# Third product of a three-stage network: one pass over the weights per token group instead of two, weights of four pairs read back from DRAM, and a one-pass PReLU on ScalarE

## The chip, the cores and the metric

The kernel runs on one core of a Trainium2 chip. The time is device microseconds of one execution; lower is better. The engines are TensorE (PE; PEld is its weight load), VectorE (DVE), ScalarE (ACT), GpSimd (POOL) and SyncE (SP), which issues nearly all DMAs. Each engine works through its own list of instructions in order.

## The reference

Decayed causal attention (4 batches, 8 heads, 576 tokens, 64 channels) gives a matrix x of 2304 tokens by 512 channels. Two feed-forward layers follow:

```python
h = x @ w_in;  g = h * sigmoid(1.702 * h);   x = g @ w_out      # first layer: products 1 and 2
h = x @ w_in;  g = max(h, 0) + alpha * min(h, 0);  g @ w_out    # second layer: products 3 and 4
```

with d_model = 512, d_ff = 2048, and alpha one number per column of h, that is per partition of the transposed h that the kernel holds. The result keeps the precision of float32.

## The kernel before

Every operand of a matmul is split in two float32r halves ("hi" by a cast, "lo" by a subtraction), and each product is three matmuls (hi·hi, hi·lo, lo·hi). All matmuls run at 128 rows of weights and 256 to 512 columns.

The order of all instructions is not written by hand. Each operation is given to a planner with its possible engines, its duration by a cost formula, what it reads and writes, and a priority; the planner places, again and again, the operation that can start first, and hands out buffers of the pools as they come free. What it emits is fixed: at run time each engine follows its list, and a late result delays whatever stands behind it. `a_sub` (lo halves, sums and differences) lets the planner choose GpSimd or VectorE; `a_copy` (hi halves) ScalarE or VectorE; `hold` ties an operation to a place in the plan.

The stages after the attention, with the times of their first matmuls in the profile:

- Product 1 (L1151), interleaved with the attention, up to 367 us. The last 768 tokens of it go through the **tail** (367 to 437 us): a Strassen-Winograd scheme (`pair`), seven products of 6 matmuls with 384 columns in place of eight. VectorE there also makes sums and differences of weights (td, tb) and prepares the weights of product 2.
- Product 2 (L1395), 437 to 627 us. Its first matmuls are placed between those of the tail. Its operands go through the tiles lh and ll (hi and lo) and lx.
- **Product 3** (L1174), 627 to 810 us, again `pair`: three groups of 768 tokens, and eight pairs of weight blocks. A pair's weights (7 combinations, hi and lo) fill one slot of the pool wS, which has 6 slots of 1,792 KB. Weights TS[0] to TS[7] are made one after the other. As only six fit, the groups are gone through twice: groups 0, 1, 2 with pairs 0 to 3, then groups 2, 1, 0 with pairs 4 to 7. The operands of a group (`group_x`: four loads of y1scr, four sums and differences at L1480, seven casts and seven subtractions) are made anew at each change of group: five times, since group 2 stands twice in a row. They lie in two pools of 3 and 4 slots.
- Product 4 (L1568), from 810 us. While product 3 runs, the weights of W2[0] to W2[2] are prepared for it.

In `pair`, three banks of PSUM are taken out of a pool of six: products 1 and 2 go to ba, 6, 7 and 4 to bb, 5 and 3 to bd, with copies (c1, u2, c5, by ScalarE at L512) and additions (by VectorE at L1203) between them. Each of the four outputs then goes through `prelu`: two ScalarE passes, relu(-h) and relu(h) (L1188, L1189), and one VectorE instruction (L1192) that adds the first, times -alpha, to the second. For the outputs o11 and o21 the passes read the bank itself; for o22 and o12 an addition has brought h to SBUF first. A bank comes free for a later product when its last reader is done.

Of the kernel before, what the change touches and what calls it, by code (L numbers as in the profile page):

```python
# [7 lines left out]
F32 = mybir.dt.float32  # L8
F32R = mybir.dt.float32r
# [15 lines left out]
SLAG = 1000.0  # L25
# [222 lines left out]
def kernel(  # L248
# [249 lines left out]
    def c_dve(n, fast=False):  # L498
        return n / (1.92 if fast else 0.96) + 68.0
# [668 lines left out]
    def product(j, x, weights, out, st, pri):  # L1168
        rd, wt = weights(TIDX[j])

        def mm(e):
            for c in range(2):
                for i, (a, b) in enumerate(((0, 0), (0, 1), (1, 0))):
                    nc.tensor.matmul(  # L1174
                        out.ap[:, :XH], wt(a, c), x.ap[:, b, c, :],
                        start=(st and c == 0 and i == 0), stop=(c == 1 and i == 2), skip_group_check=True,
                    )

        plan.add([("PE", 6 * c_mm(XH))], mm, [*rd, (x, (0, 0)), (x, (0, 1))], [out], pri)

    def prelu(o, src, mi, vp):

        tm = Buf(p_tm)
        ps = src is not None
        read = lambda: src.ap[:, :XH] if ps else o.ap

        def two(e):
            nc.scalar.activation(tm.ap, read(), AF.Relu, scale=-1.0)  # L1188
            nc.scalar.activation(o.ap, read(), AF.Relu)  # L1189

        plan.add([("ACT", 2 * c_act(XH, ps))], two, [src] if ps else [], [tm, o], vp)
        plan.add([("DVE", c_dve(XH), 0.0, True)], lambda e: nc.vector.scalar_tensor_tensor(o.ap, tm.ap, alpha_sb[:, mi:mi + 1], o.ap, op0=ALU.mult, op1=ALU.add), [tm, b_alpha], [o], vp)  # L1192

    def pair(weights, x, tmp, p_o, store, pri, vp, ms=None):
# [35 lines left out]
        store(o12, 1, 0, vp)  # L1230
        product(4, x[4], weights, bb, False, pri)
        fin(o21, bb, 0)
        store(o21, 0, 1, vp)

    def tail():
# [117 lines left out]
    for x, t in pend:  # L1353
        chunk2(x)
        advance(t)
    tail()


# [84 lines left out]
    for p in range(NPAIR):  # L1443
# [14 lines left out]
        for j, (n, src, sb_, o) in enumerate((  # L1458
# [5 lines left out]
            halves(n, src, sb_, lambda sw=sw, q=q, n=n: sw.ap[:, q:q + n], lambda sw=sw, q=q, n=n: sw.ap[:, WSLOT // 2 + q:WSLOT // 2 + q + n], sw, j, pri)  # L1464

    PART = (0, 0, 1, 2, 2, 2, 2)

    def group_x(t0, pri):
        rd = [(b_y1, (i, d)) for i in crossing(t0, GRP, in_turn) for d in range(KT)]
# [11 lines left out]

        def operand(src, pool):
            xo = Buf(pool)
            halves(2 * XH, lambda: full(src), [src], lambda: flat(xo.ap[:, 0]), lambda: flat(xo.ap[:, 1]), xo, 0, pri)
            return xo

        o = {}
        o[1] = operand(a["11"], p_xs[0])
        comb(s1, a["21"], a["22"], ALU.add)
        comb(s2, s1, a["11"], ALU.subtract)  # L1490
        o[6] = operand(s2, p_xs[0])
        o[2] = operand(a["12"], p_xs[0])
        o[5] = operand(s1, p_xs[1])
        comb(a["21"], a["11"], a["21"], ALU.subtract)
        o[7] = operand(a["21"], p_xs[1])
        comb(s2, a["12"], s2, ALU.subtract)
        o[3] = operand(s2, p_xs[1])
        o[4] = operand(a["22"], p_xs[1])
        return o

    n_it = 0
    for half in range(2):
        for gi in range(len(groups)) if half == 0 else reversed(range(len(groups))):
            t0 = groups[gi][0]
            base = 6000.0 + 100 * n_it
            if n_it != len(groups):
                x = group_x(t0, base - 150)
            for p in range(half * NPAIR // 2, (half + 1) * NPAIR // 2):
                def weights(t, p=p):
                    w = lambda: TS[p].ap.rearrange("p (a q c n) -> p a q c n", a=2, q=7, c=2)  # L1510
                    return [(TS[p], (PART[t], 0)), (TS[p], (PART[t], 1))], lambda a, c: w()[:, a, t, c, :]

                def store(src, mi, hf, vp, p=p, gi=gi, t0=t0):
                    m, s0 = p + mi * NPAIR, t0 + hf * XH
                    plan.add(DMA(P * XH * 4), lambda e: nc.sync.dma_start(h2scr[:, m, s0:s0 + XH], src.ap), [src], [(b_g2, (2 * gi + hf, m))], vp, SLAG)

                pair(weights, x, p_t, p_go, store, base + p, base + p - 50, (p, p + NPAIR))
            n_it += 1

# [12 lines left out]
    XIDX = {1: 0, 2: 2, 3: 6, 4: 1, 5: 3, 6: 4, 7: 5}  # L1532
    out_turn = [blocks[j] for j in (3, 2, 1, 0, 4)]
    g2_parts = [(i * XH, XH) for i in range(NT // XH)]
# [105 lines left out]
```

## Time and profile before

| | |
|---|---|
| time, median of 3 runs | 997.55 us (997.09 to 998.46) |
| time of the profiled execution | 997.22 us |
| its span, first to last instruction | 995.4 us |
| TensorE busy | 969.7 us (97%) |
| VectorE busy | 796.3 us (80%) |
| ScalarE busy | 635.5 us (64%) |
| granted clock of TensorE, mean | 0.997 |
| DMA | 161.27 MB, 162 GB/s |

The profiled execution's time is the span and 1.8 us around it. Busy TensorE is the union of its instructions; as matmuls overlap, a stretch is best read by how many start in it.

### The profile page before, as it was taken

How to read it: one execution, taken by the hardware profiler on the slowest of the kernel's cores; microseconds unless marked ns; L12 is line 12 of the kernel's file. 1: busy time of each engine (PE TensorE's matmuls, PEld its weight loads, DVE VectorE, ACT ScalarE, POOL GpSimd, SP SyncE). 2: the span in 40 equal slices, each digit the busy share in tenths (PEclk: the TensorE clock that was granted, in tenths of full speed). 3: DMA queues.
4: the chain of work that ended last, by engine and by line, in shares of the span. 5: the costliest groups of instructions: out<-in, count | busy, mean ns of one | idle time of the engine just before them, and what ended most of it. 6: DMA issues, size and time to landing. Idle time of an engine off the chain costs nothing.

```text
span 995.4 us, 18576 instructions
## 1 busy us (share of the span) xinstructions
PE 969.7 (97%) x6469; PEld 897.3 (90%) x6469; DVE 796.3 (80%) x1692; ACT 635.5 (64%) x1297; POOL 143.6 (14%) x277
## 2 busy tenths in 40 slices
PE   8899999999999998999999999999999999999998
PEld 6678888999998998998888988999899999999998
DVE  4778978889899789965558885688998886888976
ACT  6577744777656558866668795678988963433332
POOL 4132223443222101200000000000100000000000
PEclk9899999999999999999999999999999999999999
DMA  7666652333432125667887675544444497544423
GB/s 140 152 172 196 155 128 69 77 76 88 92 86 69 41 82 195 202 188 247 302 309 275 221 255 190 169 151 159 151 145 171 174 353 269 155 120 135 139 81 100
DMA packets 180830, 161.27 MB, mean 162 GB/s; under 512 B 99088, under 2 KB 156576, under 8 KB 179456
## 3 DMA queue, kind: packets, MB, share of 16 engines
q1 hardware_dynamic: 180720, 160.07, 52.7%
q8 instruction: 51, 0.84, 0.4%
q14 instruction: 43, 0.35, 0.1%
q10 hardware_dynamic: 16, 0.01, 0.0%
HBM read 103.51 MB, written 56.51 MB: 161 GB/s over the span
## 4 chain that ended last, share of the span: by engine, by line
PE 70%; DVE 12%; ACT 11%; issue 4%; DMA 2%; POOL 0%; SPq 0%; DVEq 0%; ACTq 0%; POOLq 0%
PE bk L1568 18%; PE bk L1395 18%; PE bk L1151 9%; PE bk L1174 9%; PE bk L1004 3%; PE bk L1072 3%; ACT lx L1188 2%; PE bk L1067 2%; PE bk L1027 2%; ACT lx L1189 2%; DVE bk L942 1%; PE bk L928 1%; ACT lx L512 1%; DMA lx<-h1scr 1%; PE bk L998 1%
## 5 line engine op out<-in xcount | busy, mean ns | idle before, releaser
L1174 PE MATMUL bk<-x,wS 128*128 128x384 f32 x1008 | 178.6, 336 | 4.3 <-DVE lx L1203 3.0
L1174 PEld LDWEIGHTS bk<-x,wS 128*128 128x128 f32 x1008 | 174.1, 188 | 8.7 <-ACT lx L512 4.0
L1151 PE MATMUL bk<-xh,w 128*128 128x256 f32 (+1 forms) x640 | 158.4, 313 | 3.4 <-ACT w L512 3.0
L1395 PE MATMUL bk<-lh,w 128*128 128x512 f32 (+1 forms) x640 | 146.9, 368 | 0.0
L1395 PEld LDWEIGHTS bk<-lh,w 128*128 128x128 f32 x640 | 112.7, 189 | 19.8
L1151 PEld LDWEIGHTS bk<-xh,w 128*128 128x128 f32 x640 | 112.0, 191 | 9.9 <-issue 3.5
L1151 PE MATMUL bk<-xl,w 128*128 128x256 f32 (+1 forms) x320 | 98.0, 306 | 1.5 <-DVE xl L517 1.5
L512 ACT CAST x<-x 128x768 fp32r<-128x768 f32 (+2 forms) x73 | 60.3, 857 | 58.2 <-PE bk L1568 43.8
L517 DVE TENSOR_TENSOR ll<-lx,lh 128x512 fp32r<-128x512 f32 (+1 forms) x79 | 50.7, 642 | 49.5 <-PE bk L1395 43.3
L942 DVE CUSTOM_DVE_ANT_0 bk<-bk,mask 128x512 f32<-128x512 f32 (+4 forms) x160 | 75.1, 490 | 12.1 <-PE bk L928 5.2
L1085 ACT ACTIVATE e<-bk 128x384 f32<-128x384 f32 (+3 forms) x192 | 62.0, 393 | 34.8 <-PE bk L1072 18.5
L517 DVE TENSOR_TENSOR x<-x,x 128x768 fp32r<-128x768 f32 (+2 forms) x73 | 70.1, 981 | 16.7 <-ACT x L512 16.0
L1395 PE MATMUL bk<-ll,w 128*128 128x512 f32 (+1 forms) x320 | 81.3, 368 | 0.1
L1192 DVE SCALAR_TENSOR_TENSOR lx<-lx,alpha_sb 128x384 f32<-128x384 f32 x96 | 61.7, 651 | 13.4 <-ACT lx L1189 12.6
L1568 PE MATMUL bk<-wS,x 128*128 128x256 f32 x567 | 70.6, 283 | 0.0
L1568 PEld LDWEIGHTS bk<-wS,x 128*128 128x128 f32 x567 | 69.2, 192 | 0.0
L1568 PE MATMUL bk<-wS,lh 128*128 128x256 f32 x378 | 68.7, 283 | 0.0
L1395 PEld LDWEIGHTS bk<-ll,w 128*128 128x128 f32 x320 | 57.0, 189 | 10.1 <-DVE ll L517 0.3
L1362 ACT ACTIVATE lx<-lx 128x512 f32<-128x512 f32 (+1 forms) x80 | 46.8, 588 | 29.6 <-DVE ll L517 26.7
L512 ACT CAST lh<-x 128x768 fp32r<-128x768 f32 (+3 forms) x38 | 31.6, 857 | 51.1 <-PE bk L1568 43.2
L1151 PEld LDWEIGHTS bk<-xl,w 128*128 128x128 f32 x320 | 61.1, 191 | 2.3 <-DVE xl L517 1.9
L1568 PEld LDWEIGHTS bk<-wS,lh 128*128 128x128 f32 x378 | 59.0, 192 | 0.0
(231 smaller groups left out, 2128.6 us busy)
## 6 DMA issues: line engine op xcount, KB each, us to landing
h2scr<-lx SPq DMA_DIRECT2D x96, 192.0 KB
wraw<-in_moe_w_in_dram SPq DMA_DIRECT2D x32, 512.0 KB
wraw<-in_moe_w_out_dram SPq DMA_DIRECT2D x32, 512.0 KB
lx<-h1scr SPq DMA_DIRECT2D x64, 256.0 KB
x<-h2scr SPq DMA_DIRECT2D x32, 512.0 KB
w2scr<-wS SPq DMA_DIRECT2D x5, 1792.0 KB
x<-y1scr SPq DMA_DIRECT2D x20, 384.0 KB
h1scr<-gg SPq DMA_DIRECT2D x48, 128.0 KB
```

Of the source, the lines that this page charges most:

```text
L512: nc.scalar.copy(dst, src)
L517: E[e].tensor_tensor(dst, a, b, op=ALU.subtract)
L942: plan.add([("DVE", c_dve(c1 - c0))], lambda e, pm=pm, c0=c0, c1=c1, mk=mk, m0=m0, col=col, f0=f0: nc.vector.tensor_tensor_reduce(pm.ap[:, ...
L1004: nc.tensor.matmul(pb[hh].ap[:, c0:c1], vr.ap[:, t, hh, :], e32.ap[:, hh, e0:e0 + m], start=st, stop=sp, skip_group_check=True,)
L1072: nc.tensor.matmul(pss[hh].ap[:w, o_:o_ + m], x.ap[r, a:a + w], y.ap[r, s0 - q0:n], start=i == 0, stop=i == 3, skip_group_check=True)
L1085: plan.add([("ACT", c_act(x1 - x0, True))], lambda e, hh=hh, pss=pss, e32=e32, w=w, x0=x0, x1=x1: nc.scalar.activation(e32.ap[:w, hh, :x1 ...
L1151: nc.tensor.matmul(ph.ap[:, :n], w.ap[:, a, c, :], x[c // 2].ap[:, c % 2, :n], start=(c == 0 and j == 0), stop=(c == KT - 1 and j == 2))
L1174: nc.tensor.matmul(out.ap[:, :XH], wt(a, c), x.ap[:, b, c, :], start=(st and c == 0 and i == 0), stop=(c == 1 and i == 2), skip_group_chec ...
L1192: plan.add([("DVE", c_dve(XH), 0.0, True)], lambda e: nc.vector.scalar_tensor_tensor(o.ap, tm.ap, alpha_sb[:, mi:mi + 1], o.ap, op0=ALU.mu ...
L1362: plan.add([("ACT", c_act(n))], lambda e: nc.scalar.activation(g.ap[:, :n], raw.ap[:, :n], AF.Gelu_apprx_sigmoid), [raw], [g], pri)
L1395: nc.tensor.matmul(py[d].ap[:, :n], w[:, a, d * P:(d + 1) * P], (lo if x else h).ap[:, :n], start=(k == 0 and (a, x) == (0, 0)), stop=(k = ...
L1568: nc.tensor.matmul(py[j].ap[:, t * HF:(t + 1) * HF], x.ap[:, q:q + P], w[:, o, a, :], start=(k == 0 and t == 0 and c == 0), stop=(k == NPA ...
```

## The change

- **Once per group.** Product 3 goes once through groups 0, 1, 2, with all eight pairs in each, in turned order: 0 to 7, then 2 to 7, 0, 1, then 4 to 7, 0 to 3. `group_x` runs three times in place of five.
- **Weights read back.** During group 0, TS[0] to TS[3] are copied to a DRAM tensor tscr (four DMAs of 1,792 KB, gated by the last product of pairs 0, 2, 4, 6). Groups 1 and 2 read two of them back each, into slots that have come free. TS[6] and TS[7] take the slots of TS[0] and TS[1], and are made during group 0.
- **Operand slots.** Two more slots (p_xe) lie in lh and ll, which product 2 has left. Group 1's operands 1 and 6 go there; a table SLOT says where each goes.
- **PReLU.** One ScalarE pass r = relu(-h) (now L1195) and one VectorE instruction h + (1 - alpha) r (L1196); alpha is turned into 1 - alpha once. For o11 and o21 VectorE reads h from the bank.
- **No GpSimd** for operations planned after the tail (`late`).
- Product 4 takes its token blocks in the order 0 to 4 (before: 3, 2, 1, 0, 4).

```diff
+    SLOT = ({1: 0, 6: 0, 2: 0, 5: 1, 7: 1, 3: 1, 4: 1}, {1: 2, 6: 3, 2: 0, 5: 0, 7: 1, 3: 1, 4: 1}, ...)
+    p_xe = [st(nm, F32R, LH, [4 * XH], 0, after=[p_str[q]]) for nm, q in (("lh", "qh"), ("ll", "ql"))]
...
     def a_sub(n):
+        if late:
+            return [("DVE", c_dve(n), 0.0, True)]
         return [("POOL", c_pool(n), 0.0, True), ("DVE", c_dve(n), BS + WS * n, True)]
...
-        def two(e):
-            nc.scalar.activation(tm.ap, read(), AF.Relu, scale=-1.0)
-            nc.scalar.activation(o.ap, read(), AF.Relu)
-        plan.add([("ACT", 2 * c_act(XH, ps))], two, [src] if ps else [], [tm, o], vp)
-        plan.add([("DVE", c_dve(XH), 0.0, True)], lambda e: nc.vector.scalar_tensor_tensor(o.ap, tm.ap, alpha_sb[:, mi:mi + 1], o.ap, op0=ALU.mult, op1=ALU.add), [tm, b_alpha], [o], vp)
+        tm = o if ps else Buf(p_tm)
+        h = lambda: src.ap[:, :XH] if ps else o.ap
+        plan.add([("ACT", c_act(XH, ps))], lambda e: nc.scalar.activation(tm.ap, h(), AF.Relu, scale=-1.0), [src] if ps else [o], [tm], vp)
+        plan.add([("DVE", c_dve(XH), 0.0, not ps)], lambda e: nc.vector.scalar_tensor_tensor(
+            o.ap, tm.ap, alpha_sb[:, mi:mi + 1], h(), op0=ALU.mult, op1=ALU.add
+        ), [tm, b_alpha, *([src] if ps else [])], [o], vp)
...
     tail()
+    late.append(True)
...
+    for p in range(KEPT):
+        keep.append(plan.add(DMA(P * WSLOT * 4), lambda e, p=p, x=TS[p]: nc.sync.dma_start(tscr[:, p], x.ap.bitcast(F32)), [TS[p]], [(b_ts, p)], 5000.0 + p))
...
-    for half in range(2):
-        for gi in range(len(groups)) if half == 0 else reversed(range(len(groups))):
-            if n_it != len(groups):
-                x = group_x(t0, base - 150)
-            for p in range(half * NPAIR // 2, (half + 1) * NPAIR // 2):
+    for gi in range(len(groups)):
+        x = group_x(t0, base - 150, gi)
+        for n_p in range(NPAIR):
+            p = (2 * gi + n_p) % NPAIR
+            if gi and n_p >= NPAIR - 2:
+                TS[p] = Buf(wS)
+                plan.add(DMA(P * WSLOT * 4), lambda e, p=p, x=TS[p]: nc.sync.dma_start(x.ap.bitcast(F32), tscr[:, p]), [(b_ts, p)], [TS[p]], base + n_p - 5)
...
+            if gi == 0 and n_p % 2 == 0:
+                hold(keep[n_p // 2], o)
```

The instructions of each engine stand in another order afterwards. Three places follow: the change of group (on two engines), the weights TS[6], and the tail.

TensorE, at the change from group 0 to the next group. In the names, bk is a bank, x, lh and ll hold operands, and wS_… is a weight slot. Before, slot 5505 is that of pair 3 of group 0, and 5813 of pair 0 of group 1:

```order
L1174 MATMUL bk_85<-x_6594,wS_5505 128x384 x6
L1174 MATMUL bk_90<-x_6558,wS_5813 128x384 x6
L1174 MATMUL bk_88<-x_6639,wS_5505 128x384 x6
L1174 MATMUL bk_91<-x_6643,wS_5505 128x384 x6
L1174 MATMUL bk_89<-x_6558,wS_5813 128x384 x6
L1174 MATMUL bk_90<-x_6594,wS_5813 128x384 x6
```

And now, with 5239 the slot of pair 7 of group 0, and 5345 of pair 2 of group 1:

```order
L1183 MATMUL bk_93<-x_6595,wS_5239 128x384 x6
L1183 MATMUL bk_86<-lh,wS_5345 128x384 x6
L1183 MATMUL bk_87<-x_6643,wS_5239 128x384 x6
L1183 MATMUL bk_88<-ll,wS_5345 128x384 x6
L1183 MATMUL bk_86<-x_6559,wS_5345 128x384 x6
L1183 MATMUL bk_90<-x_6641,wS_5239 128x384 x6
L1183 MATMUL bk_92<-x_6559,wS_5345 128x384 x6
L1183 MATMUL bk_90<-x_6643,wS_5239 128x384 x6
L1183 MATMUL bk_88<-x_6641,wS_5345 128x384 x6
```

The first two products of the new group read lh and ll, and its products that need an x slot of the old group come later.

VectorE, at the same change. Before (x are operand halves and their sums; lx outputs of `pair`; one of the four sums and differences of L1480 stands on GpSimd's list here):

```order
L517 TENSOR_TENSOR x_6558<-x_6537,x_6558 128x768
L1203 TENSOR_TENSOR bk_88<-bk_88,lx 128x384
L517 TENSOR_TENSOR x_6558<-x_6537,x_6558 128x768
L517 TENSOR_TENSOR x_6639<-x_6575,x_6639 128x768
L517 TENSOR_TENSOR x_6594<-x_6575,x_6594 128x768
L1480 TENSOR_TENSOR x_6537<-x_6575,x_6537 128x768
L1192 SCALAR_TENSOR_TENSOR lx<-lx,alpha_sb 128x384
L517 TENSOR_TENSOR x_6639<-x_6537,x_6639 128x768
L517 TENSOR_TENSOR x_6643<-x_6537,x_6643 128x768
L1203 TENSOR_TENSOR lx<-bk_88,lx 128x384
L1203 TENSOR_TENSOR lx<-bk_91,lx 128x384
```

And now:

```order
L523 TENSOR_TENSOR x_6595<-x_6538,x_6595 128x768
L523 TENSOR_TENSOR x_6643<-x_6538,x_6643 128x768
L1209 TENSOR_TENSOR bk_88<-bk_88,lx 128x384
L1209 TENSOR_TENSOR lx<-bk_90,lx 128x384
L1209 TENSOR_TENSOR lx<-bk_87,lx 128x384
L523 TENSOR_TENSOR x_6641<-x_6538,x_6641 128x768
L1196 SCALAR_TENSOR_TENSOR lx<-lx,alpha_sb 128x384 x2
L1495 TENSOR_TENSOR x_6538<-x_6576 128x768
L1495 TENSOR_TENSOR x_6538<-x_6538 128x768
L1495 TENSOR_TENSOR x_6576<-x_6538,x_6576 128x768
L523 TENSOR_TENSOR x_6643<-x_6538,x_6643 128x768
```

Fewer subtractions stand in a row ahead of the additions that free banks, and sums and differences, now those of group 2, stand on VectorE.

ScalarE, where the weights TS[6] go into the slot that TS[0] leaves; wc and tt hold the new weights before their split. Before (slot wS_5813):

```order
L512 COPY lx<-bk_88 128x384
L512 CAST wS_5813<-wc_536 128x512
L512 CAST wS_5813<-tt_5245 128x1024
L691 ACTIVATE wc_554<-wraw_414 128x512
L1188 ACTIVATE lx<-bk_87 128x384
L1189 ACTIVATE lx<-bk_87 128x384
L692 ACTIVATE wraw_414<-wraw_414 128x512
L512 COPY lx<-bk_92 128x384
```

And now (slot wS_5814):

```order
L1195 ACTIVATE lx<-bk_90 128x384
L518 COPY lx<-bk_87 128x384
L518 CAST wS_5814<-wc_537 128x256
L518 CAST wS_5814<-wc_555 128x512
L518 CAST wS_5814<-tt_5246 128x1024
L700 ACTIVATE wc_537<-wraw_415 128x512
L1195 ACTIVATE lx<-bk_93 128x384
L701 ACTIVATE wraw_415<-wraw_415 128x512
L518 COPY lx<-bk_86 128x384
```

In the kernel before, the slot's last readers are matmuls; now its readers include the copy of the slot to tscr. The copies out of banks (COPY) stand behind the casts in both.

TensorE, in the tail (tb and w hold weights there). Before, matmuls of product 2 (L1395) stand between the products of the tail:

```order
L1174 MATMUL bk_88<-xt_4432,tb_4409 128x384 x6
L1174 MATMUL bk_86<-xt_4366,tb_4513 128x384 x6
L1174 MATMUL bk_85<-xt_4372,tb_4513 128x384 x6
L1174 MATMUL bk_88<-xt_4327,w_944 128x384 x6
L1395 MATMUL bk_89<-lh,w_102 128x512 x2
L1395 MATMUL bk_90<-lh,w_102 128x512 x2
L1395 MATMUL bk_92<-lh,w_102 128x512 x2
L1395 MATMUL bk_87<-lh,w_102 128x512 x2
L1174 MATMUL bk_86<-xt_4418,tb_4513 128x384 x6
```

And now, at the same products:

```order
L1183 MATMUL bk_89<-xt_4432,tb_4409 128x384 x6
L1183 MATMUL bk_87<-xt_4366,tb_4512 128x384 x6
L1183 MATMUL bk_86<-xt_4372,tb_4512 128x384 x6
L1183 MATMUL bk_89<-xt_4327,w_944 128x384 x6
L1183 MATMUL bk_87<-xt_4418,tb_4512 128x384 x6
```

Ahead of the last pair's products, 20 matmuls of product 2 stood in the tail (8, 4 and 8); now 8 do, and the rest stand at its end.

## Rows read from the trace of the kernel before

**Rows 1.** Windows by stage: us, busy PE/PEld/DVE/ACT/POOL (x), PEclk, DMA, GB/s.

```profile
364.00:437.00 73.00, 70.47 (x387) 67.31 (x387) 69.19 (x123) 58.56 (x108) 10.25 (x12) 1.00 0.59 191
...
627.00:809.00 182.00, 177.72 (x1006) 173.32 (x1005) 158.90 (x268) 151.86 (x319) 10.88 (x8) 1.00 0.52 171
```

**Rows 2.** The same view, third product cut in stretches of 30 us.

```profile
660.00:690.00 30.00, 28.42 (x162) 27.63 (x161) 24.33 (x36) 23.21 (x50) 2.49 (x1) 1.00 0.43 142
690.00:720.00 30.00, 28.17 (x159) 26.94 (x158) 27.71 (x51) 26.28 (x57) 5.25 (x4) 1.00 0.47 160
720.00:750.00 30.00, 29.26 (x163) 27.83 (x162) 28.25 (x52) 26.99 (x58) 3.14 (x3) 1.00 0.47 150
750.00:780.00 30.00, 30.00 (x174) 29.90 (x174) 25.94 (x42) 25.50 (x54) 0.00 (x0) 1.00 0.44 152
780.00:809.00 29.00, 28.87 (x165) 28.06 (x164) 26.81 (x52) 24.70 (x52) 0.00 (x0) 1.00 0.75 256
```

**Rows 3.** Line L1174: duration ns min/median/max, first and last start us.

```profile
L1174 PE MATMUL bk<-x,wS x1008: 333/334/446, 627.1 to 809.6; 128*128 128x384 f32 x168
```

**Rows 4.** Timeline, TensorE, first group change: start us, us [idle <-releaser].

```profile
654.70 11.18 PE L1174 MATMUL bk<-x,wS 128*128 128x384 f32 x63
667.29 2.35 PE L1174 MATMUL bk<-x,wS 128*128 128x384 f32 x12 [1.42 <-DVE lx L1203]
```

**Rows 5.** Timeline, VectorE, first group change.

```profile
661.25 1.14 DVE L1192 SCALAR_TENSOR_TENSOR lx<-lx,alpha_sb 128x384 f32<-128x384 f32 x2
...
664.05 2.72 DVE L1192 SCALAR_TENSOR_TENSOR lx<-lx,alpha_sb 128x384 f32<-128x384 f32 x2
666.70 1.01 DVE L1203 TENSOR_TENSOR lx<-bk,lx 128x384 f32<-128x384 f32 x2
```

**Rows 6.** Timeline, GpSimd, first group change: start us, us.

```profile
663.34 2.49 POOL L1480 TENSOR_TENSOR x<-x 128x768 f32<-128x768 f32 x1 [104.95 <-DVE x L517]
```

**Rows 7.** VectorE by line and form, 627 to 809: busy, mean ns.

```profile
L1192 DVE SCALAR_TENSOR_TENSOR lx<-lx,alpha_sb 128x384 f32<-128x384 f32 x93 | 59.9, 652 | 13.4 <-ACT lx L1189 12.6
L517 DVE TENSOR_TENSOR x<-x,x 128x768 fp32r<-128x768 f32 x32 | 29.5, 952 | 3.9 <-ACT x L512 3.5
L1203 DVE TENSOR_TENSOR lx<-bk,lx 128x384 f32<-128x384 f32 x47 | 25.3, 551 | 5.1 <-PE bk L1174 4.8 <-ACT lx L1188 0.2
...
L517 DVE TENSOR_TENSOR wS<-tt,wS 128x1024 fp32r<-128x1024 f32 x5 | 6.1, 1221 | 0.5 <-ACT wS L512 0.5
...
L694 DVE CUSTOM_DVE_ANT_0 wc<-wraw,wc 128x1024 uint16<-128x1024 uint16 x6 | 4.1, 684 | 0.0
L517 DVE TENSOR_TENSOR wS<-wc,wS 128x512 fp32r<-128x512 f32 x5 | 3.4, 683 | 0.0
...
L517 DVE TENSOR_TENSOR wS<-wc,wS 128x256 fp32r<-128x256 f32 x5 | 2.1, 419 | 0.0
```

**Rows 8.** ScalarE by line and form, 627 to 809: busy, mean ns.

```profile
L512 ACT COPY lx<-bk 128x384 f32<-128x384 f32 x72 | 34.2, 489 | 5.5 <-DVE bk L1203 3.9 <-PE bk L1174 1.3
...
L1188 ACT ACTIVATE lx<-bk 128x384 f32<-128x384 f32 x47 | 23.3, 496 | 0.6 <-PE bk L1174 0.6
```

**Rows 9.** Queue of SyncE, timeline: a copy of one weight slot to DRAM.

```profile
529.80 0.32 SPq L1440 DMA_DIRECT2D w2scr<-wS  x1
```

**Rows 10.** Windows of 1 us around that copy.

```profile
531.00:532.00 1.00, 1.00 (x6) 0.84 (x5) 0.23 (x1) 0.74 (x2) 0.00 (x0) 1.00 1.06 422
...
535.00:536.00 1.00, 1.00 (x6) 0.82 (x5) 1.00 (x3) 0.75 (x3) 0.00 (x0) 1.00 0.89 297
```

**Rows 11.** Windows of 1 us, weight slots being read back.

```profile
796.00:797.00 1.00, 1.00 (x7) 0.81 (x6) 1.00 (x3) 1.00 (x3) 0.00 (x0) 1.00 0.68 149
```

**Rows 12.** Timeline, GpSimd, in the tail.

```profile
373.61 1.44 POOL L517 TENSOR_TENSOR w<-wc,w 128x512 fp32r<-128x512 f32 x1 [23.27 <-ACT w L512]
```

**Rows 13.** Timeline, VectorE, in the tail.

```profile
373.81 1.78 DVE L1285 TENSOR_TENSOR tw<-w 128x512 f32<-128x512 f32 x1
```

**Rows 14.** Timeline, TensorE, in the tail.

```profile
376.45 1.66 PE L1174 MATMUL bk<-xt,tb 128*128 128x384 f32 x8 [0.84 <-DVE got L1203]
```

More of the change, by code (lines that the diff above doesn't have):

```diff
@@ L296 @@
     SPILL = 3
+    KEPT = 4
     HF = 256
@@ L464 @@
     p_xs = (sl("x", F32R, [2, 2, XH], (1, 0, 2), (2, 0, 1), after=[wo[0]]), sl("x", F32R, [2, 2, XH], (4, 0, 2), (5, 0, 2), after=[wo[1]]))
+    SLOT = ({1: 0, 6: 0, 2: 0, 5: 1, 7: 1, 3: 1, 4: 1}, {1: 2, 6: 3, 2: 0, 5: 0, 7: 1, 3: 1, 4: 1}, {1: 0, 6: 1, 2: 0, 5: 0, 7: 1, 3: 1, 4: 1})
     old = [p_str["qr"], p_str["qg"]]
+    p_xe = [st(nm, F32R, LH, [4 * XH], 0, after=[p_str[q]]) for nm, q in (("lh", "qh"), ("ll", "ql"))]
+    for x in p_xe:
+        x.make = lambda i, f=x.make: f(i).rearrange("p (a b c) -> p a b c", a=2, b=2)
     p_t = {n: st("lx", F32, LX, [XH], *(3072 * j + 1536 * i for i in range(2)), after=old) for j, n in enumerate(("c1", "u2", "c5"))}
@@ L1177, in mm @@
                     )
[L1179 removed]
+        return plan.add([("PE", 6 * c_mm(XH))], mm, [*rd, (x, (0, 0)), (x, (0, 1))], [out], pri)
     def prelu(o, src, mi, vp):
[L1183 removed]
         ps = src is not None
[L1185 to L1192 removed]
+        tm = o if ps else Buf(p_tm)
[4 more added lines that the diff above has]
+        ), [tm, b_alpha, *([src] if ps else [])], [o], vp)
     def pair(weights, x, tmp, p_o, store, pri, vp, ms=None):
@@ L1230, in pair @@
         store(o12, 1, 0, vp)
-        product(4, x[4], weights, bb, False, pri)
+        last = product(4, x[4], weights, bb, False, pri)
         fin(o21, bb, 0)
         store(o21, 0, 1, vp)
+        return last
     def tail():
@@ L1383 @@
     Y = []
+    less = plan.add([("DVE", c_dve(NM, True))], lambda e: nc.vector.tensor_scalar(alpha_sb, alpha_sb, -1.0, 1.0, op0=ALU.mult, op1=ALU.add), (), [b_alpha], 2500.0)
     for i, (t0, n) in enumerate(in_turn):
@@ L1405 @@
             Y.append(o)
+            if len(Y) == 8:
+                hold(less, o)
         for d in range(KT):
@@ L1480, in comb, with operand @@
             plan.add(a_sub(2 * XH), lambda e: E[e].tensor_tensor(full(dst), full(x), full(y), op=op), [x, y], [dst], pri)
-        def operand(src, pool):
-            xo = Buf(pool)
+        def operand(src, j):
+            pool = (*p_xs, *p_xe)[SLOT[gi][j]]
+            xo = o[j] = Buf(pool)
             halves(2 * XH, lambda: full(src), [src], lambda: flat(xo.ap[:, 0]), lambda: flat(xo.ap[:, 1]), xo, 0, pri)
-            return xo
         o = {}
-        o[1] = operand(a["11"], p_xs[0])
+        operand(a["11"], 1)
@@ L1489, in group_x @@
         comb(s1, a["21"], a["22"], ALU.add)
         comb(s2, s1, a["11"], ALU.subtract)
-        o[6] = operand(s2, p_xs[0])
-        o[2] = operand(a["12"], p_xs[0])
-        o[5] = operand(s1, p_xs[1])
+        operand(s2, 6)
+        operand(a["12"], 2)
+        operand(s1, 5)
         comb(a["21"], a["11"], a["21"], ALU.subtract)
-        o[7] = operand(a["21"], p_xs[1])
+        operand(a["21"], 7)
         comb(s2, a["12"], s2, ALU.subtract)
-        o[3] = operand(s2, p_xs[1])
-        o[4] = operand(a["22"], p_xs[1])
@@ L1499, in group_x @@
-        return o
-    n_it = 0
-    for half in range(2):
-        for gi in range(len(groups)) if half == 0 else reversed(range(len(groups))):
-            t0 = groups[gi][0]
-            base = 6000.0 + 100 * n_it
-            if n_it != len(groups):
-                x = group_x(t0, base - 150)
-            for p in range(half * NPAIR // 2, (half + 1) * NPAIR // 2):
[L1509 to L1518, printed above, removed]
+        operand(s2, 3)
@@ new lines, in group_x, with weights, store @@
+        operand(a["22"], 4)
+        return o
+    for gi in range(len(groups)):
+        t0 = groups[gi][0]
+        base = 6000.0 + 100 * gi
+        x = group_x(t0, base - 150, gi)
[4 more added lines that the diff above has]
+                plan.add(DMA(P * WSLOT * 4), lambda e, p=p, x=TS[p]: nc.sync.dma_start(x.ap.bitcast(F32), tscr[:, p]), [(b_ts, p)], [TS[p]], base + n_p - 5)
+            def weights(t, ts=TS[p]):
+                w = lambda: ts.ap.rearrange("p (a q c n) -> p a q c n", a=2, q=7, c=2)
+                return [(ts, (PART[t], 0)), (ts, (PART[t], 1))], lambda a, c: w()[:, a, t, c, :]
+            def store(src, mi, hf, vp, p=p, gi=gi, t0=t0):
+                m, s0 = p + mi * NPAIR, t0 + hf * XH
+                plan.add(DMA(P * XH * 4), lambda e: nc.sync.dma_start(h2scr[:, m, s0:s0 + XH], src.ap), [src], [(b_g2, (2 * gi + hf, m))], vp, SLAG)
+            o = pair(weights, x, p_t, p_go, store, base + n_p, base + n_p - 50, (p, p + NPAIR))
+            if gi == 0 and n_p % 2 == 0:
+                hold(keep[n_p // 2], o)
@@ L1532 @@
     XIDX = {1: 0, 2: 2, 3: 6, 4: 1, 5: 3, 6: 4, 7: 5}
-    out_turn = [blocks[j] for j in (3, 2, 1, 0, 4)]
+    out_turn = [blocks[j] for j in range(5)]
     g2_parts = [(i * XH, XH) for i in range(NT // XH)]
```

10 lines of the change are left out of this document (6 added, 4 removed).

## The prediction

> **What bounds the kernel now.** I read the windows by stage first, for TensorE's share [rows 1]. It works through all but a few us of every stage at a granted clock of 1.00, so an idle engine elsewhere is worth nothing by itself: a gain can only come from gaps between matmuls. Next come the windows of the third product [rows 2] with the line of its matmuls [rows 3]. Both kernels issue the same 1008 matmuls there. They start from 627.1 to 809.6 us, and with the last one's 0.33 us the stage takes 182.8 us. The stretch 750 to 780 holds 174 matmuls in 30.00 us at full busy time, which makes 172.4 ns each; 1008 of them would take 173.8 us. So 9.0 us are lost in this stage, and the count of each window says where: 660 to 690 holds 162 (27.9 us of work, 2.1 lost), 690 to 720 holds 159 (2.6 lost), 720 to 750 holds 163 (1.9 lost), 750 to 780 loses nothing, 780 to 809 holds 165 (0.6 lost). The remaining 1.8 us lie before 660.
>
> Then I read why. On TensorE's timeline a run of 63 matmuls starts at 654.70 [rows 4]. At 172.4 ns they are issued by 665.56, yet the next starts at 667.29, released by an addition of L1203 that had to free a bank: about 1.7 us lost. On VectorE those additions stand behind two L1192 instructions that took 2.72 us together, where the same pair took 1.14 us a little earlier [rows 5]. On GpSimd one sum of the new operands (L1480) ran from 663.34 to 665.83 [rows 6], and the slow pair overlaps it. So while GpSimd reads its two operands, VectorE's instruction with two operands in SBUF is held, and the delay goes straight into the bank that TensorE needs. The same GpSimd instruction runs in the window from 690 to 720, which has GpSimd busy for 5.25 us and the largest loss [rows 2]. These two windows lose 4.7 us.
>
> **The change, part by part.** The sum is made against the profiled execution, 997.2 us (995.4 of span and 1.8 around it); the median of the runs, 997.55, is 0.3 above it.
>
> *No GpSimd behind the tail, and fewer switches.* GpSimd's 10.88 us in the stage go [rows 1], and with them the hold. What VectorE takes over is sums of 768 columns, for which the nearest row is the 768-column subtraction, 952 ns [rows 7]; but three operand sets are made in place of five and more, so it drops 14 such subtractions (13.3 us) and six sums (5.7 us) and takes back about 2.8 us: some 16 us less of 158.9. That VectorE is idle more is worth nothing. What counts is what stands ahead of the bank-freeing additions at a change of group: five subtractions in a row became fewer, with operands 1 and 6 made ahead, and a held pair (1.58 us too long) became a 0.95 us sum. If every such hold is replaced by a sum on the path, the gain is at least 2 x (1.58 - 0.95) = 1.3 us; at most it is all 4.7. Six or more products (1.03 us each) lie between the release of a slot and the need for it in the new order, so I take 4.0.
>
> *Where VectorE will be fullest.* A group is now 336 matmuls, 57.9 us. Its eight pairs cost VectorE 8 x (4 x 0.652 + 3 x 0.551) = 34.1 us [rows 7]. Group 0 also makes group 1's operands, 11 instructions of 0.95 (10.5 us), and two weight slots. A slot costs 1.22 + 0.68 + 0.42 in lo halves, two unpackings of 0.68, and seven short ones near 0.42: 6.6 us, and two make 13.3. That is 57.9 us; consecutive instructions overlap by about 0.09 (two of 551 take 1.01 [rows 5]), 8.2 us for 91 of them, which leaves 49.7 of 57.9, 86%. Group 1 is lower. Group 2 carries three slots for product 4 (19.9) and its first operands (8 x 0.95 = 7.6): 61.6, less 9.0, is 52.6, or 91%. The window that lost nothing was at 25.94 of 30, 86%; the one at 28.25 of 30, 94%, lost 1.9 [rows 2]. So group 0 should run clean and the end of group 2 lose somewhat. Of the 1.9 us at 720 to 750 I take 0.4 as gained and the rest as moved to the end; the bounds are -1.0 and +1.9.
>
> *The one-pass PReLU.* One ScalarE pass of about 0.50 us [rows 8] goes from each of 96 outputs: ScalarE falls from 151.9 to some 105 us. VectorE keeps its 96 instructions, and its idle time ahead of them, 12.6 us behind the second pass [rows 7], shrinks. But for o11 and o21 the bank is now held until VectorE has read it. No row shows this instruction with a bank as input. The nearest ones: the addition that reads a bank takes 551 ns at 384 columns, and between the 419 ns of 256 columns and the 952 ns of 768, both from SBUF, one would read 552 [rows 7]. So I charge nothing for the bank; the bounds are a gain of 0.5 us (a second pass of 0.50 gone ahead of each release, seldom the last one) and a loss of 0.5 us.
>
> [...]
>
> *The copies to DRAM and back.* Four slots of 1,792 KB (1.835 MB) are written, and read four times. The copies out delay whoever refills the slot: the casts of TS[6] and TS[7], on ScalarE's list ahead of the copies out of banks. The trace has one such copy, issued at 529.80 [rows 9], with 422 GB/s after one us and 297 still at 535 [rows 10]; at 297 it takes 6.2 us. The slowest stretch of weights arriving had 149 GB/s [rows 11]: 12.3 us. If the casts are placed where a landing after 6.2 us just clears, the slow case holds ScalarE by 6.1 us; TensorE has about two products (2 us) in hand, so it loses 4 per copy, 8 for the two refills that must wait. The DMA share in the stage is 0.52 [rows 1], so I take 0.3 and keep 0 and 8. The four reads have some 28 products (28 us) between the slot's release and its first use, against 12.3 at worst: hidden, at nothing. If that cover went, each would cost up to 12.
>
> *The tail.* Here too GpSimd holds VectorE: a subtraction of 1.44 us [rows 12], beside a 512-column difference that took 1.78 [rows 13] where the like takes 0.68 [rows 7], and TensorE then waits 0.84 us for an addition [rows 14]. In the new order that goes, but VectorE takes over three differences of 256 columns (3 x 0.42 = 1.3), and 12 of the 20 matmuls of product 2 that filled gaps between the tail's products now stand behind them. VectorE is at 69.2 of 73.0 us in this stretch, TensorE at 70.5 [rows 1], so the filler mattered. I take 0; the bounds are a gain of 2 and a loss of 3.
>
> Sum: 4.0 + 0.4 + 0 - 0.3 + 0 = 4.1 us. A half us more I allow for the 1.8 lost before 660, where GpSimd also stands on the list. That makes 4.5: 997.2 - 4.5 = 992.7.
>
> **The rivals.**
> *A, all gaps close.* If every loss of the stage came from GpSimd's holds and the ScalarE passes, 9.0 go, and about 2 in the tail: 986.2. For it: the window without GpSimd lost nothing. Against: 780 to 809 had no GpSimd either and lost 0.6, and 720 to 750 was full on VectorE.
> *B, VectorE is the gate.* With the tail's filler gone its 1.3 us of differences show, and group 2 loses at the rate of the 94% window, 1.9 per 30 us, or 3.7 less the 0.6 already there: 997.2 - 4.7 + 1.3 + 3.1 = 996.9. Against: 91% was reckoned, not 94.
> *C, slower: ScalarE held by a slot's copy.* As worked out above, the casts of TS[6] and TS[7] stand at the head of its list until the copy has landed, with the copies out of banks behind them: 992.7 + 8 = 1000.7. It decides once a copy lands later than about 8 us after its issue (6.2 and the two products in hand). For it: one list, and a queue shared with the operand loads. Against: the one copy of the trace.
> *D, the holds are not the cause.* If the slow pairs return without GpSimd, nothing is gained but moved: about 997.
>
> **How the numbers follow.** A measurement here tells 0.2% from no change, so faster is below 995.6 and slower above 999.5. The forecast has 0.60 (its own range 989 to 995.4), A 0.12, B 0.13, C 0.11, D 0.04. Faster: 0.60 + 0.12 and a little of B, 0.73. Slower: C and a share of B in which the tail loses its 3, 0.13. Same: 0.14. The range runs from 987.5, which leaves out half of A, to 998.0, which takes in B and D and leaves out C.
>
> **What would show it.** Right: no GpSimd instruction in product 3; pairs of the PReLU instruction near 1.1 us at the changes of group; about 174 matmuls per 30 us through groups 0 and 1, a few less at the end of group 2; ScalarE near 105 us in the stage; the PReLU instruction that reads a bank near 652 ns. Wrong: ScalarE idle behind a DMA ahead of the weight casts (C); waits of TensorE for L1209 that are as long as before while VectorE is over 94% (B), or gaps between the tail's last products; TensorE waiting on the DMA of a slot read back.

## The result, and the profile after

The changed kernel took 982.82 us (median of 4 runs, 981.63 to 984.30); the kernel before, run beside it, 997.32 us (996.12 to 998.46). The ratio is 0.9855, with a 95% interval of 0.9836 to 0.9875: 14.5 us faster. The forecast was 992.7, in a range of 987.5 to 998.0. The direction was right; the size was wrong by a factor of three, and the time lies outside the range.

The profiled execution of the changed kernel has a span of 982.5 us against 995.4, 12.9 less; it was the slowest of the four (984.30), so the two traces show somewhat less than the 14.5 us between the medians. Both kernels issue the same 6469 matmuls, so the two traces can be laid beside each other on TensorE, stage by stage, each stage from its first matmul to the next one's:

| stage, on TensorE | before | after | gain |
|---|---|---|---|
| the first 400 matmuls (61.9 us before) | 61.9 | 55.4 | 6.6 |
| from there to the tail | 305.2 | 305.8 | -0.6 |
| tail and first part of product 2 | 87.7 | 86.1 | 1.5 |
| rest of product 2 | 172.3 | 173.2 | -0.9 |
| product 3, first to last matmul | 182.5 | 176.2 | 6.3 |
| product 4 | 181.5 | 181.5 | 0.0 |

Half of the gain lies in the first 62 us, where the change has no product at all. The two small losses (0.6 and 0.9) are of the size by which one execution differs from another: the kernels of the experiments that were made from the changed one took 304.6 to 305.4 and 172.0 to 172.8 us there. The three gains come again in the one of them that moves nothing but alpha's load: 55.8, 86.3 and 176.5 us.

**The start.** ScalarE's timeline of the kernel before, around 40 us (start, duration, line, tiles, count, idle time before it and its releaser):

```profile
36.40 0.66 ACT L692 ACTIVATE wraw<-wraw 128x512 int32<-128x512 uint32 x1
42.59 0.21 ACT L660 ACTIVATE alpha_sb<-alpha_sb 128x16 f32<-128x16 f32 x1 [5.54 <-DMA alpha_sb<-in_moe_alpha_dram]
42.71 0.60 ACT L512 CAST w<-wc 128x512 fp32r<-128x512 f32 x1
```

and TensorE's, in the same stretch:

```profile
43.37 0.38 PE L1151 MATMUL bk<-xh,w 128*128 128x256 f32 x1 [2.99 <-ACT w L512]
```

ScalarE's timeline of the changed kernel at the same place:

```profile
38.06 0.62 ACT L518 CAST w<-wc 128x512 fp32r<-128x512 f32 x1 [1.01 <-DVE wc L703]
```

The 0.21-us negation of alpha stood at the head of ScalarE's list and waited 5.54 us for the load of alpha. Behind it stood the cast of the weights for the first matmuls of product 1, and TensorE waited for that. alpha isn't needed before the third product, almost 600 us later. The one-pass PReLU needs 1 - alpha in place of -alpha, so the change takes this instruction off ScalarE's list and makes the number on VectorE in product 2. The cast now starts 4.65 us earlier.

**The third product.** Windows of the changed kernel (us; busy PE, PEld, DVE, ACT, POOL with counts; PEclk; DMA; GB/s), the stage and then two stretches of 30 us, as [rows 1, 2]:

```profile
620.00:797.00 177.00, 176.48 (x1013) 175.09 (x1013) 141.13 (x254) 108.08 (x216) 0.00 (x0) 1.00 0.70 245
653.00:683.00 30.00, 30.00 (x175) 30.00 (x174) 24.34 (x44) 20.45 (x41) 0.00 (x0) 1.00 0.88 305
...
743.00:773.00 30.00, 29.89 (x173) 29.58 (x172) 25.55 (x54) 19.64 (x41) 0.00 (x0) 1.00 0.84 302
```

VectorE falls from 158.9 to 141.1 us and ScalarE from 151.9 to 108.1, both close to what the prediction reckoned. Both changes of group (from 676 and from 732 us) pass without a stall. TensorE's timeline shows it, as [rows 4] did for the stalls:

```profile
623.08 53.21 PE L1183 MATMUL bk<-x,wS 128*128 128x384 f32 x305
676.13 1.20 PE L1183 MATMUL bk<-lh,wS 128*128 128x384 f32 x6
...
732.50 49.45 PE L1183 MATMUL bk<-x,wS 128*128 128x384 f32 x282
782.21 14.83 PE L1183 MATMUL bk<-x,wS 128*128 128x384 f32 x84 [0.26 <-DVE lx L1209]
```

No line from 623.08 to 732.50 has idle time before it. 305 matmuls start in a row between 623.08 and 676.13, 173.9 ns each. That is taken as the pace of this code without a wait: 1008 of them take 175.3 us, so the stage of before lost 7.5 of its 182.8 us, and the changed one, 176.5 with its last matmul, loses 1.2.

**Copies and PReLU.** ScalarE's group of casts that wait for a slot to be written out (busy, mean ns, idle before and its releaser), as in [rows 8]:

```profile
L518 ACT CAST wS<-wc 128x256 fp32r<-128x256 f32 x5 | 2.0, 405 | 0.3 <-DMA tscr<-wS 0.2
```

And VectorE's two kinds of PReLU instruction in the same stage, as in [rows 7], the first with h in a bank:

```profile
L1196 DVE SCALAR_TENSOR_TENSOR lx<-lx,alpha_sb,bk 128x384 f32<-128x384 f32 x47 | 27.9, 609 | 5.9 <-ACT lx L1195 5.9
L1196 DVE SCALAR_TENSOR_TENSOR lx<-lx,alpha_sb 128x384 f32<-128x384 f32 x47 | 27.8, 612 | 1.3 <-ACT lx L1195 0.4
```

The copies to DRAM hold ScalarE for 0.2 us in all: rival C did not come. It was near, though: the casts that waited start at 640.51, 7.8 us after the copy's issue at 632.67, where the prediction reckoned 6.2 us for a landing and put C at about 8. The instruction that reads h from a bank takes 609 ns, the one that reads it from SBUF 612. Before, with GpSimd at work beside some of them, the mean was 652.

### The profile page after: what moved, and what is told of

The parts are those of the page before. It is cut to its first block, busy times and chain, and to the rows that moved or that the text cites. A ratio compares the mean times of both kernels' runs of the same rounds, so it can differ in the third digit from the quotient of the medians.

```text
span 982.5 us, 18432 instructions
## 1 busy us (share of the span) xinstructions
PE 963.1 (98%) x6469; PEld 895.1 (91%) x6469; DVE 778.0 (79%) x1689; ACT 587.2 (60%) x1187; POOL 118.4 (12%) x258
## 4 chain that ended last, share of the span: by engine, by line
PE 81%; DVE 8%; ACT 6%; issue 2%; DMA 1%; POOL 1%; ACTq 0%; DVEq 0%; POOLq 0%
PE bk L1183 21%; PE bk L1404 19%; PE bk L1586 18%; PE bk L1160 10%; PE bk L1013 3%; PE bk L1081 3%; PE bk L1076 2%; PE bk L1036 2%; DVE bk L951 1%; PE bk L937 1%; ACT e L1094 1%; DVE el L523 1%; PE bk L926 1%; PE bk L1007 1%; DMA lx<-h1scr 1%
## 5 line engine op out<-in xcount | busy, mean ns | idle before, releaser
L1183 PE MATMUL bk<-x,wS 128*128 128x384 f32 x912 | 160.8, 335 | 0.5 <-DVE lx L1209 0.3
L1183 PEld LDWEIGHTS bk<-x,wS 128*128 128x128 f32 x912 | 158.1, 188 | 1.9 <-DVE lx L1209 1.0
L518 ACT CAST x<-x 128x768 fp32r<-128x768 f32 (+3 forms) x57 | 47.2, 857 | 63.0 <-PE bk L1586 47.2
L523 DVE TENSOR_TENSOR x<-x,x 128x768 fp32r<-128x768 f32 (+3 forms) x59 | 57.0, 982 | 16.4 <-ACT x L518 16.0
L518 ACT COPY gg<-bk 128x256 f32<-128x256 f32 (+1 forms) x78 | 32.2, 416 | 39.8 <-PE bk L1160 35.3
```

Of the source, the lines that this page charges most:

```text
L518: nc.scalar.copy(dst, src)
L523: E[e].tensor_tensor(dst, a, b, op=ALU.subtract)
L1183: nc.tensor.matmul(out.ap[:, :XH], wt(a, c), x.ap[:, b, c, :], start=(st and c == 0 and i == 0), stop=(c == 1 and i == 2), skip_group_chec ...
```

## The experiments

All kernels below were timed in five rounds beside the kernel before, whose median was 996.5 in the first group, 996.8 in the second and 996.3 in the third. The changed kernel was not timed again beside them, so a comparison with its 982.82 us carries the difference of up to 1 us between 997.32 and these medians.

**The start.** First the one instruction alone, on the kernel before (TensorE's, GpSimd's and SyncE's lists stay the same):

```diff
-    plan.add([("ACT", c_act(NM))], lambda e: nc.scalar.mul(alpha_sb, alpha_sb, -1.0), (), [b_alpha], 300)
...
+    less = plan.add([("DVE", ...)], lambda e: nc.vector.tensor_scalar(alpha_sb, alpha_sb, -1.0, None, op0=ALU.mult), (), [b_alpha], 2500.0)
```

> The kernel before with one instruction moved: the negation of alpha leaves ScalarE's list near 37 us and stands on VectorE's in product 2. Everything else keeps its order on every engine. Theory S: this instruction waited 5.5 us for the slow load of alpha at the head of ScalarE's list, TensorE's operands stood behind it, and its removal is the 6 us that the changed kernel is ahead before any changed product: 997.3 - 6 to 7 = about 991, and TensorE's matmuls from 46 us on start 6 us earlier. Rival R: the lead comes from transfers that happen to land earlier in one execution; then 997, no change. Rival G: TensorE gets the 6 us but gives them back in later waits of the attention; then 994 to 997.

991.42 us (990.46 to 991.91); ratio 0.9946, interval 0.9933 to 0.9960: 5.1 us of the 14.5. TensorE has 400 matmuls behind it at 55.15 us, in place of 61.9, and at the tail the lead is still 6.3 us; the third product is as before (182.5). So it is theory S, and nothing is given back (against G).

Then the same instruction put back into the changed kernel:

```diff
+    plan.add([("ACT", c_act(NM))], lambda e: nc.scalar.mul(alpha_sb, alpha_sb, -1.0), (), [b_alpha], 300)
...
-    ... tensor_scalar(alpha_sb, alpha_sb, -1.0, 1.0, ...)
+    ... tensor_scalar(alpha_sb, alpha_sb, 1.0, 1.0, ...)
```

> The changed kernel with the negation of alpha put back on ScalarE at the same place as before (VectorE then makes 1 + (-alpha) in product 2); all other orders as in the changed kernel. Theory S: ScalarE waits some 5.5 us again for the load, 982.8 + 6 to 7 = about 989, and the third product keeps its 176.5 us. Rival R: 983, since the lead has nothing to do with the instruction.

989.23 us (987.45 to 990.78); ratio 0.9924, interval 0.9908 to 0.9940: 6.4 us more than the changed kernel (6.9 by the ratios). ScalarE's timeline of this kernel has the wait again:

```profile
41.67 0.22 ACT L670 ACTIVATE alpha_sb<-alpha_sb 128x16 f32<-128x16 f32 x1 [4.51 <-DMA alpha_sb<-in_moe_alpha_dram]
```

From both sides, this one instruction is worth 5 to 7 us. Its third product takes 176.5 us and its rest of product 2 172.3, not 173.2.

Why was the load so late? SyncE's queue in the kernel before (start, duration):

```profile
37.60 1.82 SPq L721 DMA_DIRECT2D raw<-in_q_dram  x4
39.46 0.46 SPq L659 DMA_DIRECT2D alpha_sb<-in_moe_alpha_dram  x1
```

It was issued at 39.46, behind loads of q and k; ScalarE had been waiting since 37. The next kernel is the one before with alpha in coarser pieces:

```diff
-    nc.sync.dma_start(alpha_sb, alpha.rearrange("(m p) -> p m", p=P))
+    nc.sync.dma_start(alpha_sb, alpha.rearrange("(p m) -> p m", p=P))
```

> The kernel before with alpha loaded as 16 consecutive numbers per partition (128 pieces of 64 bytes) in place of 2048 pieces of 4 bytes; the numbers then belong to other columns of h, the work and all orders are the same. Theory S, part two: the wait is long because the load is cut so finely: it lands some us earlier and most of the 5.5 us wait goes, 991 to 993. Rival Q: the load lands late because it is issued late, behind the weights in the same queue; then the wait stays and the time is 997.

994.11 us (992.63 to 996.92); ratio 0.9976, interval 0.9966 to 0.9987: 2.4 us. On ScalarE:

```profile
40.76 0.22 ACT L660 ACTIVATE alpha_sb<-alpha_sb 128x16 f32<-128x16 f32 x1 [3.05 <-DMA alpha_sb<-in_moe_alpha_dram]
```

SyncE issues the load at 38.87 in this kernel. From its issue to the negation it is 1.9 us in place of 3.1 (3.2 to 3.6 in the five other profiled kernels that load the small pieces and negate there), but 3.05 us of waiting stay. Both readings hold a part: cutting the load into small pieces cost 1.2 us or somewhat more, and the larger part is the place of its issue in the queue. In the changed kernel the load still stands there, with nobody waiting; the fourth kernel moved it to product 2:

```diff
+            if len(Y) == 4:
+                hold(a_load, o)
```

> The changed kernel with the load of alpha moved from 38 us to the start of product 2; otherwise the same orders. If the 2048 small pieces also slow the loads of weights beside them, the start gains something more: 980 to 982.5. If only the waiting instruction mattered: 982.8, no change.

983.35 us (983.21 to 984.00); ratio 0.9868, interval 0.9853 to 0.9883: no difference from the changed kernel that these runs can show. So the pieces cost the other loads nothing that shows; only the wait mattered.

**The parts of the third product.** Three parts were taken alone: GpSimd shut out behind the tail (G), the one-pass PReLU (P), once per group with slots read back (O). In each of the three, alpha's negation stays on ScalarE at the start.

G alone, on the kernel before:

```diff
     def a_sub(n):
+        if late:
+            return [("DVE", c_dve(n), 0.0, True)]
...
     tail()
+    late.append(True)
```

> The kernel before with GpSimd shut out of what is planned behind the tail, nothing else; the wait for alpha at the start stays, and the third product still changes its operands five times. Theory H (GpSimd's sums hold VectorE at the changes of group): the two long stalls of 1.6 and 1.8 us and what follows them go, and 1.5 us in the tail, so 996.5 - 5 to 6 = about 991, of which 4.5 in the third product. Rival L (what mattered is VectorE's load, and the changes of group themselves): VectorE takes on some 8 us more of the same work in the stage, the additions still come late, and the third product keeps 182 us or gets longer: 995 to 998.

992.30 us (991.51 to 994.08); ratio 0.9960, interval 0.9947 to 0.9972: 4.5 us. The kernel before has the second of the two stalls here, on TensorE:

```profile
698.96 2.35 PE L1174 MATMUL bk<-x,wS 128*128 128x384 f32 x12 [1.61 <-DVE lx L1203]
```

With GpSimd shut out the third product begins like this:

```profile
625.32 84.76 PE L1178 MATMUL bk<-x,wS 128*128 128x384 f32 x480
```

The two stalls at the changes of group are gone although the changes themselves stay, which is what theory H said (the order of VectorE's list changes too, and its share was not taken apart). But shorter waits come up in their place (0.1 to 0.5 us of idle TensorE between 695 and 802, most behind ScalarE's copies), and the third product ends at 179.4 us.

P alone, on the kernel before: the `prelu` of the change, and 1 - alpha made from -alpha in product 2.

> The kernel before with the one-pass PReLU alone (negation still on ScalarE at the start). Theory P: the waits for ScalarE's copies out of banks (L512) in 720 to 750, some 2 us, came from its second PReLU pass standing ahead of them and go: 996.5 - 2 to 3 = about 994; the two stalls at the changes of group stay. Rival: the bank is held until VectorE has read it, and the additions come later: 996 to 998. [...]

990.86 us (990.83 to 991.92); ratio 0.9945, interval 0.9932 to 0.9957: 6.0 us, more than either theory gave. What was expected to stay, the stalls at the changes, went too, with GpSimd at work in the same place. GpSimd's timeline of this kernel at the first change of group:

```profile
661.62 2.44 POOL L1480 TENSOR_TENSOR x<-x,x 128x768 f32<-128x768 f32 x1 [103.25 <-ACT lx L1186]
```

VectorE's beside it, and later:

```profile
662.27 1.14 DVE L1187 SCALAR_TENSOR_TENSOR lx<-lx,alpha_sb,bk 128x384 f32<-128x384 f32 x2
...
708.98 2.70 DVE L1187 SCALAR_TENSOR_TENSOR lx<-lx,alpha_sb 128x384 f32<-128x384 f32 x2
```

TensorE's:

```profile
627.02 84.50 PE L1174 MATMUL bk<-x,wS 128*128 128x384 f32 x486
712.73 90.46 PE L1174 MATMUL bk<-x,wS 128*128 128x384 f32 x516 [1.20 <-ACT lx L512]
```

The pair of PReLU instructions that runs beside GpSimd's sum now reads a bank, and takes 1.14 us, as undisturbed; the pair of before, with both inputs in SBUF, took 2.72 [rows 5, 6]. At the second change it is the same (a pair at 691.41 that reads a bank takes 1.13 us beside a sum from 690.76 to 693.20), and TensorE goes through 486 matmuls without a wait. So at both changes GpSimd finds nothing to hold. The hold itself is not gone: at 708.98 a pair of PReLU instructions with both inputs in SBUF takes 2.70 us while GpSimd works (1.30 us from 708.96 on and 0.94 from 710.34), an addition on VectorE and a copy on ScalarE stand behind it, and TensorE waits 1.20 us for that copy. Which pair stands beside GpSimd's sum is decided by the order that the planner found.

O alone, on the kernel before: the loop, `group_x`, SLOT, p_xe and the copies of the change, with the old `prelu`, GpSimd allowed and alpha as before.

> The kernel before with the third product gone through once per group alone, slots read back and the two operand slots in lh and ll with it: two-pass PReLU, GpSimd allowed, negation at the start. Theory H: GpSimd still makes sums at the changes, so at least one long stall stays and the gain is 2 to 3 us: about 994. Rival L: fewer subtractions ahead of the additions and less work on VectorE are enough, the third product comes to about 178 us: 996.5 - 5 = 991 to 992.

991.30 us (990.74 to 992.35); ratio 0.9948, interval 0.9935 to 0.9962: 5.5 us, as rival L gave. GpSimd still makes one sum at a change of group (689.45 to 691.56), and it holds a subtraction of VectorE (1.68 us in place of 0.95); but two additions stand ahead of that, and TensorE's longest wait in the stage is 0.4 us.

Each part alone gives 4.5 to 6 us, but together, without the start, they give about 8. So they were also taken away one at a time. Without G:

```diff
-    late.append(True)
```

> The changed kernel with GpSimd allowed again behind the tail. Theory H: its sums return to the changes of group and hold VectorE, 982.8 + 3 to 5 = 986 to 988, in the third product and the tail. Rival L: with three operand sets in place of five and ScalarE relieved there is slack for it, so the third product stays at 176.5 us and only the tail may lose its 1.5: 983 to 984.5.

983.68 us (983.52 to 985.68); ratio 0.9874, interval 0.9861 to 0.9888: about the changed kernel's time. In its profiled execution the third product is 1.2 us shorter than the changed kernel's, and the tail 2.7 longer. Rival L was right on the third product: it does not get longer. The window over the tail, columns as above, of the changed kernel:

```profile
354.00:430.00 76.00, 74.27 (x414) 71.94 (x413) 73.64 (x138) 60.55 (x111) 6.67 (x8) 1.00 0.60 192
```

And of this one:

```profile
354.00:430.00 76.00, 72.86 (x399) 69.22 (x398) 71.07 (x126) 59.20 (x110) 10.22 (x12) 1.00 0.58 183
```

TensorE starts 15 matmuls fewer in the same 76 us.

Without P, the changed kernel with the two-pass `prelu` and alpha negated on VectorE:

> The changed kernel with the two-pass PReLU of before (negation of alpha still on VectorE in product 2). Theory O (the parts overlap: each of them alone takes most of the same 8 us of losses out of the third product): it lengthens by 0 to 2 us, 982.8 to 985. Rival A (the parts add up: the one-pass PReLU alone took 4.9 us out of the third product): 982.8 + 4 to 5 = 987 to 988.

982.29 us (982.15 to 982.99); ratio 0.9862, interval 0.9848 to 0.9875: no loss that shows. Theory O, at its lower end.

Without O, G and P together on the kernel before:

> The kernel before with the one-pass PReLU and without GpSimd behind the tail, the third product still gone through twice and alpha negated on ScalarE at the start. Theory O: the third product comes to 176 to 178 us, hardly under the 177.6 of the PReLU alone, and the tail gains 1 to 2.5: 988 to 990. Rival A: 182.5 - 4.9 - 3.1 = 174.5 us and below it the floor of 174.7: 986 to 987.

988.40 us (988.23 to 991.27); ratio 0.9928, interval 0.9916 to 0.9941. Theory O again. With the start's 5 to 7 taken off this is the changed kernel's time.

That fills the table. Products 3 and 4 together, from TensorE's first matmul of product 3 to its last, in one profiled execution each (four profiled kernels have the changed kernel's lists there and give 357.0 to 358.0, so differences of 1 us tell nothing); and the tail with the first part of product 2. The new order of product 4's blocks goes with O:

| parts | products 3 and 4 | gain | tail |
|---|---|---|---|
| none | 364.0 | | 87.7 |
| G | 360.9 | 3.1 | 86.5 |
| P | 358.4 | 5.6 | 88.7 |
| O | 357.8 | 6.2 | 88.3 |
| G and P | 357.8 | 6.2 | 86.2 |
| G and O | 357.4 | 6.6 | 86.1 |
| P and O | 356.5 | 7.5 | 88.8 |
| all three | 357.7 | 6.3 | 86.1 |

In the third product the parts replace each other: there were 7.5 us to have, and O or P alone takes most of them; G alone takes 3.1. In the tail it is G alone that counts, about 2 us.

**Two versions more.** GpSimd shut out of product 2 only, to have 86.1 and 356.5 at once:

```diff
+    late.clear()
     W2 = {}
```

> The changed kernel with GpSimd shut out of product 2 alone, and allowed from the third product on. The changed kernel with GpSimd back everywhere had 175.05 us in the third product (1.2 less) but 2.7 more in the tail. If the two are independent: tail as in the changed kernel, third product 175, so 982.8 - 1 = about 981.6. Rival: the gain in the third product comes from another plan and goes with it: 983.

981.96 us (981.07 to 982.93); ratio 0.9856, interval 0.9841 to 0.9871. Its profiled execution has 86.1 in the tail and 356.9 for products 3 and 4, but neither the 356.9 nor the 0.9 us less than 982.82 is to be told apart from the changed kernel by these runs.

GpSimd shut out of the tail too:

```diff
-    tail()
     late.append(True)
+    tail()
```

> The changed kernel with GpSimd shut out of the tail as well: eight differences of 256 columns go to VectorE, 8 x 0.42 = 3.4 us on an engine that is at 73.6 of 76 us there. If VectorE is the gate of the tail: 982.8 + 1 to 3 = 984 to 986. If the waits come from GpSimd holding VectorE there too (the 1.2 us before an addition at 379): 981 to 982.

984.63 us (983.81 to 986.41); ratio 0.9886, interval 0.9873 to 0.9900. The tail has 88.6 us. Inconclusive on the cause: the wait at 379 shrank from 1.22 to 0.71 us, and in a new one TensorE waits 2.04 us for the copy of ScalarE at 421.56, which stands behind a load on ScalarE's list rather than behind VectorE:

```profile
420.49 0.66 ACT L700 ACTIVATE wc<-wraw 128x512 f32<-128x512 f32 x1 [1.04 <-DMA wraw<-in_moe_w_out_dram]
...
421.56 0.47 ACT L518 COPY u2t<-bk 128x384 f32<-128x384 f32 x1
```

## Why the prediction was wrong

- **The term that is missing: the start.** The part on the one-pass PReLU counted the passes that go and left out the negation of alpha that the change takes off ScalarE's list. It lasts 0.21 us, but its price was its wait: 5.54 us on ScalarE, 3 us of idle TensorE at once and about 6 in all. Taken away it gave 5.1, put back it cost 6.4. This is most of the error, and the trace of before had it: one row of ScalarE's waits, for a DMA that nobody else wanted. The prediction read the stages from the tail on and left out the start, where no product is changed.
- **The windows.** The claim of 9.0 us lost, 1.8 of them before 660, came out of counts by window, which hold the matmuls that reach over an edge at both ends. By starts in a row the pace is 173.9 ns and 7.5 us were lost; the half us allowed for before 660 had no ground, since 222 matmuls start there from 627.11 on without a wait. (4.1 and a half also make 4.6, not 4.5.)
- **The changes of group** were right in their cause and nearly in size. Forecast 4.0 of 4.7 us; by starts the two stalls and the short waits right behind them come to 4.0, and none is left. G alone takes both away, and the held pairs beside GpSimd's sums show how they came about. What the prediction had wrong is that GpSimd's removal is what pays: P takes them away with GpSimd still there, and O, too, has no stall at its changes. Where the other two parts are in, the removal gains nothing in the third product (356.5 without it, 357.7 with it).
- **720 to 750** was mis-sized: forecast 0.4 of 1.9 gained, since the work was thought to move to the end of group 2 at 91% of VectorE. Over group 0 (621 to 679) VectorE came to 50.0 of 58 us, the 86% of the forecast; over group 2 (738 to 797) to 50.4 of 59, 85% and not 91%. TensorE loses about 0.7 us there by starts, in two waits for VectorE's additions (at 761 and 782).
- **The PReLU at a bank** at no charge: right, 609 against 612 ns (47 of each in the stage).
- **The copies** at 0.3: right, 0.2 us of waiting. Rival C did not come, with the copies landing just in time; the reads back stalled nobody (none of TensorE's waits in the stage is for a DMA).
- **The tail** at 0, between a gain of 2 and a loss of 3: it gained 1.5 in the profiled pair and about 2 over all kernels with G against those without. The filler of product 2 that left the tail did not matter as much as thought; what of GpSimd's removal makes the gain there was not taken apart.
- **The rivals.** A came closest in the third product (1.2 us of 7.5 are left), but no rival had the start.

The sum as measured: about 6 at the start, 6.3 in the third product and 1.5 to 2 in the tail, 14 of the 14.5. Why P alone gives 5.6 in products 3 and 4 is settled for the two changes of group only; how its shorter ScalarE list and the bank it reads share the rest was not taken apart.

## What to carry to other kernels

Ask of every instruction that a change removes what it waits for, not only how long it lasts, and read it where it stands in its engine's list, however far from the stage that the change is about: a tiny preparation whose input comes by a DMA can block an engine for everything behind it (here 0.21 us of work with 5.54 us of wait). Such preparations belong behind the first work that doesn't need them. When several edits attack the same few us of waits, try each alone and each left out: their gains don't add up, and one of them may be paying for nothing.

## What the runs showed of the hardware

- A two-input VectorE instruction with both inputs in SBUF that starts while GpSimd runs a two-input sum is held (2.72 against 1.14 us for a pair, beside a sum of 2.49 us); with one of its inputs in a bank it isn't (1.14 us beside a GpSimd sum of 2.44 us, and 1.13 beside a second one; in the same kernel a pair with both inputs in SBUF takes 2.70 beside GpSimd instructions of 1.30 and 0.94 us).
- 8 KB in 2048 pieces of 4 bytes were usable 3.1 to 3.6 us after the issue (six executions), in 128 pieces of 64 bytes 1.9 us after it (one). The fine pieces did not slow the program when nobody waited for them (983.35 against 982.82 us, no difference).
